# The last layer's weight product joins the order that is planned at build time; the low parts of converted weights move from POOL to DVE

## The chip, the cores and the metric

The kernel runs on one core of a Trainium2 chip. The metric is the device time of one execution in microseconds (us). Three runs of the kernel before took 1078.37, 1080.1 and 1088.2 us, so its median is 1080.1 us. The engines are named as in the profile: PE multiplies matrices (PEld is its weight load), DVE, ACT and POOL do elementwise work, SP issues the DMAs.

## The reference

```
x = attention(q, k, v)            # 4 batches, 8 heads, 576 positions, head size 64, rotary q and k, softmax
x = x / rms(x) * rms_g            # 2304 tokens x 512
x = (silu(x @ w_gate) * (x @ w_val)) @ w_out       # 512 -> 1536 -> 512
x = (((x @ w1) * (x @ w2)) @ w3) @ w_out2          # 512 -> 1024 -> 1024 -> 512
```

The weights arrive as 64-bit floats and are converted on the chip. A product of two float32 matrices is made of three passes (`PASS`): every operand is held as a rounded high part and a low part (the operand less its high part), and the passes are high x high, high x low and low x high.

## The kernel before

**Stages.** The attention (from 0 to about 320 us of the profiled execution) has an order of its own, written out by hand, with the conversion of the first six weight tiles inside it. What follows it is cut here into stages that the text calls B to F.

- B, to 474 us: the gate and value products of the first chunks of tokens (`products_b`, PE line L1059), the gate (`gate_b`), their product with w_out (`second_b`, L1085), and the conversion of 30 more weight tiles (`one_unit`, `convert`, `unit_out`), two per step. A conversion is one ACT operation, two DVE operations (L1117, L1119), one store, and the split into high part (ACT) and low part (`tt` with `pool=True`, on POOL). The rms normalisation of the other tokens (`n_out`) lies in B too.
- C, to 649 us: gate and value products of the other chunks with fewer block products (`block_products`, L1302). Sums and differences of weight blocks are made on POOL (`weights`, `comb`), their splits on ACT and DVE. There are 12 batches of two units.
- D, to 749 us: the product with w_out for those chunks (L1449).
- E, to about 927 us: the products with w1 and w2 (L1302 again), 12 batches of two jobs, 24 jobs. The product of both, u, goes to memory as `uD`.
- F, to the end: first w3 @ w_out2 is made, so that two layers become one. w3 is loaded (`w3_load`), transposed on PE (`w3_trans`, L1552), split, and multiplied with the eight splits `woc` of w_out2 (`w3_prod`, L1563). Then six chunks of u are loaded and split (`load_us`), multiplied with the eight tiles `wp` (L1605, 72 matmuls a chunk), copied out of PSUM and stored.

**The order.** From B to E every operation is handed to `Plan` with its engine, an estimate of its duration and what it reads and writes. At build time `Plan.place` goes through the operations as a list scheduler: PE keeps the order of the program; on ACT, DVE, POOL and SP the operation with the earliest due time goes first among those that are ready. Each engine then has a fixed order. The planner of the kernel before knows nothing that joins DVE and POOL: the two run side by side in its model. Stage F is not in the plan. It is written behind `plan.run()` and `man.close()`, and the framework's own scheduler puts its instructions in order, among the last ones of E as well.

**Buffers.** SBUF is addressed in kilobytes per partition (`mv(address, shape)`), and an address used again waits for the last use of what lay there. PSUM has eight banks that are handed out in turn (`bank`, `pbank`). In E the sums of chunk pairs 0, 1 and 2 lie at `XSA`, `XSB` and `XSC`; the last batch is jobs (3, 1, 1) and (3, 1, 2) and so uses `XSB` and `XSC`, not `XSA`.

**Lines.** L986 and L987 are ACT in `act`, L992 is `tt` (DVE or POOL), L995 is `stt` (DVE), L998 is `dma`, L1117 and L1119 are the two DVE operations of `convert`, L1538 and L1539 are ACT and DVE of stage F's `split`, L885 is a copy in the attention's first steps.

Of the kernel before, what the change touches and what calls it, by code (L numbers as in the profile page):

```python
# [60 lines left out]
SUMS_D, SUMS_E = (72, 78), (194, 200)  # L61
G_AT = (0, 6, 12, 18, 24)
XSC = (84, 90, 96, 182, 188, 72, 78)
ARENAS = ((0, 54), (54, 78), (78, 122), (122, 182), (182, 204))

C_BATCHES = ([[(0, 0), (1, 0)], [(0, 1), (1, 1)]] + [[(f_, 0), (f_, 1)] for f_ in range(2, 10)] + [[(10, 0), (11, 0)], [(10, 1), (11, 1)]])
# [58 lines left out]
class Plan:  # L125
# [4 lines left out]
    def __call__(self, eng, dur, fn, rd=(), wr=(), dep=(), pre=(), due=None, kb=0):  # L130
        o = Op()
        o.eng, o.dur, o.fn, o.kb, o.due, o.pre, o.wr = eng, dur, fn, kb, due, list(pre), wr
        o.i = len(self.ops)
        o.dep = set(dep)
        for acc, w in [(a, 0) for a in rd] + [(a, 1) for a in wr]:
            sp, lo, hi = acc
            if sp not in self.log and isinstance(sp, View):
                for v, log in list(self.log.items()):
                    if isinstance(v, View) and v.lo < sp.hi and sp.lo < v.hi:
                        self.entry.setdefault(sp, set()).update(self.used[v] - {o})  # L140
                        self.over.add(v)
                        del self.log[v]
                        if v.lo < sp.lo or sp.hi < v.hi:
                            self.log[v] = log
            assert sp not in self.over
            if w:
                o.dep |= self.entry.get(sp, set())
            old = self.log.setdefault(sp, [])
            self.used.setdefault(sp, set()).add(o)
            for e in old:  # L150
                if e[0] < hi and lo < e[1] and (w or e[3]) and e[2] is not o:
                    o.dep.add(e[2])
            if w:
                old[:] = [e for e in old if not (lo <= e[0] and e[1] <= hi)]
            old.append((lo, hi, o, w))
        self.ops.append(o)
        return o
# [27 lines left out]
    def place(self, nxt, by, pe):  # L185
        free = dict.fromkeys(("PE", "ACT", "DVE", "POOL", "SP", "X"), 0.0)
        left = {o: len(o.dep) for o in self.ops}
        ready = {e: [] for e in free}
        when = {}
        wire = 0.0  # L190
        self.seq = {e: [] for e in free}
        pe_at = 0

        def release(o):
            when[o] = max([0.0] + [(d.end if o.eng != "X" else d.start) + self.lat(d, o) for d in o.dep])
            ready[o.eng].append(o)

        for o in self.ops:
            if not left[o]:
                release(o)  # L200
        n = 0
        while n < len(self.ops):
            best = None
            for e, r in ready.items():
                if not r:
                    continue
                if e == "PE":
                    o = pe[pe_at]
                    if left[o]:
                        continue  # L210
                    c = (max(free[e], when[o]), o)
                else:
                    t = max(free[e], min(when[o] for o in r))
                    if e == "SP":
                        t = max(t, wire - 3.0)
                    o = min((o for o in r if when[o] <= t), key=lambda o: (by[o], o.i))
                    late = [d for d in r if t < when[d] < t + o.dur and by[d] < by[o] and t + o.dur > max(by[d], when[d] + 0.3)]
                    if late:
                        o = min(late, key=lambda o: when[o])
                        t = when[o]  # L220
                    c = (t, o)
                if best is None or c[0] < best[0]:
                    best = c
            t, o = best
            ready[o.eng].remove(o)
            if o.eng == "PE":
                pe_at += 1
            o.start, o.end = t, t + o.dur
            free[o.eng] = o.end
            if o.kb:  # L230
                wire = max(wire, o.end) + o.kb / 300
                o.end = max(wire, o.end + o.kb / 300) + 1.8
            self.seq[o.eng].append(o)
            n += 1
            for x in nxt[o]:
                left[x] -= 1
                if not left[x]:
                    release(x)
# [28 lines left out]
def kernel(  # L267
# [881 lines left out]
    def unit_out(hi, lo, ph, pl, put, ks, t):  # L1149
        dma(256, put, [ks], lambda: t.ap, [t.part()])  # L1150
        act(hi, [ph], lambda: t.ap, [t.part()], 512)
        tt(lo, [pl], lambda: t.ap, lambda: f(hi()), [t.part(), ph], 512, pool=True)


    NT2 = (NCH - 2) * NR
# [125 lines left out]
    bk = [0]  # L1281
    banks = []

    def bank():
        bk[0] += 1
        i = (bk[0] - 1) % 8
        return (lambda: banks[i][:, 0:CH]), key("bank", i)

    first_c = [None]

# [223 lines left out]
    jobs += [(g, s, P) for g in range(1, NJ // 2) for s in range(2) for P in range(NP2)]  # L1514
    G = {}
    todo = [jobs[k:k + 2] for k in range(0, len(jobs), 2)]
    for batch in todo:
        for g, s, _ in batch:
            if (g, s) not in ws:
                ws[g, s] = wsE(g, s)  # L1520
# [2 lines left out]
            for step in run:  # L1523
                step(i)

    plan.run()
    man.close()


    gtiles, w3s = Ring(G_AT, (DM,)), Ring([a + 2 * i for a in CW for i in range(7)], (512,))  # L1530
    woc, w3T, w3c = {}, {}, {}

    def pbank():
        bk[0] += 1
        return banks[(bk[0] - 1) % 8]

    def split(hi, lo, src, eng=nc.vector):
        nc.scalar.copy(out=hi, in_=src)  # L1538
        eng.tensor_tensor(out=lo, in0=src, in1=f(hi), op=ALU.subtract)  # L1539

    def w3_load(j):
        for h in range(2):
            t = w3c[j, h] = w3s.new().ap
            nc.sync.dma_start(out=t, in_=w3D[:, j, h])

    def w3_trans(j):
        t = w3T[j] = [gtiles.new((NJ, 128), F32R).ap for _ in range(2)]
        for h in range(2):
            src = w3c.pop((j, h))
            p_ = pbank()  # L1550
            for c in range(4):
                nc.tensor.transpose(p_[:, c * 128:(c + 1) * 128], src[:, c * 128:(c + 1) * 128], idn)  # L1552
            split(t[0][:, 4 * h:4 * h + 4], t[1][:, 4 * h:4 * h + 4], p_.rearrange("p (c n) -> p c n", c=4))

    wp = {}

    def w3_prod(j):
        p_ = pbank()
        i = 0
        t = w3T.pop(j)  # L1560
        for c in range(NJ):
            for a, b_ in PASS:
                nc.tensor.matmul(p_, lhsT=t[a][:, c], rhs=woc[c][:, b_], start=(i == 0), stop=(i == 3 * NJ - 1))  # L1563
                i += 1
        o = wp[j] = mv(XSC[j] if j < 7 else XSB[1], (2, 512), F32R).ap
        split_s(o[:, 0], o[:, 1], p_, UP**-2)

    u_ring = Ring(XSB[2:6] + XSA * 4, (2, 2, CH), F32R)

    def load_us(i):  # L1570
        us = []
        for g in range(NJ // 2):
            o = u_ring.new().ap
            nc.sync.dma_start(out=f(o[:, 1]), in_=uD[:, 2 * g:2 * g + 2, i * CH:(i + 1) * CH])
            split(o[:, 0], o[:, 1], f(o[:, 1]))
            us.append(o)
        return us

    for j in range(2):
        w3_load(j)  # L1580
    for j in range(NJ):
        woc[j] = mv(XSA[j] if j < 7 else XSB[0], (3, 512), F32R).ap
        nc.sync.dma_start(out=f(woc[j][:, 2]), in_=woD[:, j])
    for j in range(NJ):
        split(woc[j][:, 0], woc[j][:, 1], f(woc[j][:, 2]))
    w3_trans(0)
    for j in range(NJ):
        if j == NJ - 3:
            nus = load_us(0)
        if j + 2 < NJ:  # L1590
            w3_load(j + 2)
        if j + 1 < NJ:
            w3_trans(j + 1)
        w3_prod(j)


    for i in range(NCH):
        us = nus
        if i + 1 < NCH:
            nus = load_us(i + 1)  # L1600
        ac = [pbank() for _ in range(NR)]
        for j in range(NJ):
            for o in range(NR):
                for s, (a, b_) in enumerate(PASS):
                    nc.tensor.matmul(ac[o], lhsT=us[j // 2][:, a, j % 2, o * 128:(o + 1) * 128], rhs=wp[j][:, b_],  # L1605
                                     start=(j == 0 and s == 0), stop=(j == NJ - 1 and s == 2))
        for o in range(NR):
            t = gtiles.new().ap
            if o == 1:
                nc.vector.tensor_copy(out=t, in_=ac[o])  # L1610
            else:
                nc.scalar.copy(out=t, in_=ac[o])
            g, w = divmod(i * NR + o, 9)
            if w < 8:
                b_, r = 2 * g + w // 4, w % 4
                nc.sync.dma_start(out=out[b_ * S:b_ * S + 512, :].rearrange("(p r) n -> p r n", r=4)[:, r, :], in_=t)
            else:
                for b_ in range(2):
                    e = (2 * g + b_ + 1) * S
                    nc.sync.dma_start(out=out[e - 64:e, :], in_=t[b_ * 64:b_ * 64 + 64, :])  # L1620


# [48 lines left out]
```

## Time and profile before

| | us |
|---|---|
| median of three runs (1078.37 to 1088.2) | 1080.1 |
| profiled execution | 1086.88 |
| its span, first to last instruction | 1085.1 |
| PE busy | 1053.2 (97%) |
| DVE busy | 726.5 (67%) |
| ACT busy | 631.5 (58%) |
| POOL busy | 397.4 (37%) |

The span is what the trace holds; the execution is 1.8 us longer. Busy time is the time in which an engine has an instruction under way, and the rest of the span is idle time. The granted clock is the share of TensorE's full clock (2.4 GHz) that the chip allowed; 0.50 is 1.2 GHz.

### The profile page before, as it was taken

The page shows a single profiled execution, that of the slowest core. Times are in us where ns is not written, and L with a number is a line of the kernel's source. Part 1 is how long each engine was busy: PE and PEld are TensorE (multiplying, and loading weights), DVE is VectorE, ACT ScalarE, POOL GpSimd, SP SyncE. Part 2 cuts the span into 40 slices and gives each one's busy share as a digit, 9 for nine tenths or more (in the row PEclk, how much of TensorE's full clock was granted, in tenths as well). Part 3 has the DMA queues.
Part 4 walks back from the last instruction along what each step waited for, and adds up shares of the span by engine and source line. Part 5 has one row for each costly group of instructions (what it writes and reads, how often), then busy time and mean ns, then how long its engine had stood idle before and what let it go on. Part 6 is the DMA issues. An engine that isn't in the chain of part 4 may idle for free.

```text
span 1085.1 us, 18628 instructions
## 1 busy us (share of the span) xinstructions
PE 1053.2 (97%) x6525; PEld 1017.2 (94%) x6525; DVE 726.5 (67%) x1235; ACT 631.5 (58%) x1414; POOL 397.4 (37%) x509
## 2 busy tenths in 40 slices
PE   7699999999999999999999999999999999899997
PEld 6699999999999899999999999999999999788886
DVE  6999999999987865878787786433745344523220
ACT  4699999898977554557666674323544334322220
POOL 7668897889623444632231230012421110000000
PEclk9899999999999999999999999999999999999999
DMA  6387877777649886369998866653222128304441
GB/s 184 85 214 198 229 186 178 186 193 193 171 158 318 256 283 226 107 200 355 303 303 275 304 211 224 183 162 117 88 69 84 62 88 265 114 1 134 128 146 59
DMA packets 129181, 196.32 MB, mean 181 GB/s; under 512 B 19008, under 2 KB 78016, under 8 KB 129088
## 3 DMA queue, kind: packets, MB, share of 16 engines
q1 hardware_dynamic: 129088, 195.13, 59.5%
q8 instruction: 52, 0.85, 0.3%
q14 instruction: 41, 0.34, 0.1%
HBM read 110.54 MB, written 56.89 MB: 154 GB/s over the span
## 4 chain that ended last, share of the span: by engine, by line
PE 62%; DVE 1%; DMA 1%; issue 1%; ACT 0%; POOL 0%; DVEq 0%; POOLq 0%; ACTq 0%
PE ps L1302 30%; PE ps L1449 9%; PE ps L1605 9%; PE mm L1059 6%; PE ps L1563 4%; PE acc L1085 3%; DVE v L992 1%; DMA v<-x2D 0%; PE ps L1552 0%; DMA v<-uD 0%; DVE v L995 0%; POOL v L992 0%; DMA v<-woD 0%; PE xp L1186 0%; DVE v L1117 0%
## 5 line engine op out<-in xcount | busy, mean ns | idle before, releaser
L1302 PE MATMUL ps<-v 128*128 128x384 f32 x2016 | 350.9, 334 | 0.1
L1302 PEld LDWEIGHTS ps<-v 128*128 128x128 f32 x2016 | 349.3, 188 | 0.8 <-ACT ps L986 0.8
L992 POOL TENSOR_TENSOR v<-v 128x256 f32<-128x256 f32 (+2 forms) x150 | 155.7, 1053 | 400.6 <-DMA v<-x2D 108.5
L986 ACT CAST v<-v 128x256 fp32r<-128x256 f32 (+3 forms) x312 | 151.4, 508 | 149.8 <-DMA v<-uG 37.9
L992 DVE TENSOR_TENSOR v<-v 128x256 fp32r<-128x256 f32 (+3 forms) x282 | 173.6, 641 | 90.2 <-ACT v L986 89.7
L650 PE MATMUL s<-ks,qs 128*128 128x288 f32 x640 | 121.0, 315 | 14.7 <-ACT p L661 13.6
L661 ACT ACTIVATE p<-s,nm 128x576 f32<-128x576 f32 x144 | 107.4, 746 | 19.5 <-DVE nm L655 18.9
L655 DVE TENSOR_REDUCE nm<-s 128x1 f32<-128x576 f32 x144 | 108.0, 751 | 7.4 <-PE s L650 5.5
L1059 PE MATMUL mm<-v 128*128 128x384 f32 x576 | 106.5, 339 | 3.4 <-DVE v L995 2.4
L650 PEld LDWEIGHTS s<-ks,qs 128*128 128x128 f32 x640 | 90.4, 191 | 18.1 <-ACT p L661 16.1
L1059 PEld LDWEIGHTS mm<-v 128*128 128x128 f32 x576 | 101.5, 190 | 4.7 <-DVE v L995 2.6
L1449 PE MATMUL ps<-v 128*128 128x384 f32 x576 | 100.0, 334 | 0.0
L1449 PEld LDWEIGHTS ps<-v 128*128 128x128 f32 x576 | 99.9, 188 | 0.0
L1605 PE MATMUL ps<-v 128*128 128x512 f32 x432 | 98.1, 389 | 0.0
L1605 PEld LDWEIGHTS ps<-v 128*128 128x128 f32 x432 | 81.1, 188 | 16.8
L675 DVE TENSOR_TENSOR pt<-tp,pt 128x512 fp32r<-128x512 f32 x144 | 94.7, 683 | 1.3 <-ACT pt L671 0.6
L992 DVE TENSOR_TENSOR v<-ps,v 128x384 f32<-128x384 f32 x96 | 53.0, 555 | 57.4 <-PE ps L1302 56.1
L986 ACT COPY v<-ps 128x384 f32<-128x384 f32 x120 | 57.2, 479 | 52.3 <-PE ps L1302 50.8
L671 ACT CAST pt<-tp 128x512 fp32r<-128x512 f32 x144 | 82.3, 584 | 1.1 <-PE tp L667 0.2
L667 PE MATMUL tp<-idn,p 128*128 128x128 f32 x576 | 81.9, 274 | 0.9 <-DVE lt L705 0.8
L723 PE MATMUL pv<-pt,vs 128*128 128x288 f32 x512 | 80.9, 300 | 0.1
L723 PEld LDWEIGHTS pv<-pt,vs 128*128 128x128 f32 x512 | 70.9, 188 | 0.3 <-DVE pt L675 0.3
(125 smaller groups left out, 1372.6 us busy)
## 6 DMA issues: line engine op xcount, KB each, us to landing
ks<-xy SPq DMA_DIRECT2D x60, 288.0 KB, 4.9
v<-in_moe_w_dram SPq DMA_DIRECT2D x32, 512.0 KB, 6.2
v<-in_moe_w_out_dram SPq DMA_DIRECT2D x20, 512.0 KB, 6.4
qs<-xy SPq DMA_DIRECT2D x60, 160.0 KB, 2.8
uG<-v SPq DMA_DIRECT2D x24, 384.0 KB, 4.4
v<-uG SPq DMA_DIRECT2D x24, 384.0 KB, 3.8
uD<-v SPq DMA_DIRECT2D x12, 768.0 KB, 3.4
v<-uD SPq DMA_DIRECT2D x24, 384.0 KB, 4.3
```

The costliest lines, as they stand in the source:

```text
L650: nc.tensor.matmul(ps[:, hf, 0:HS], lhsT=l, rhs=r_[:, hf * HS:(hf + 1) * HS], start=(i == 0), stop=(i == n - 1))
L655: nc.vector.tensor_reduce(out=nm, in_=s_ps[p, t][:, :, 0:HS], axis=AX.XY, op=ALU.max, negate=True)
L661: nc.scalar.activation(out=pp.rearrange("p (a b) -> p a b", a=2), in_=s_ps.pop((p, t))[:, :, 0:HS], func=AF.Exp, bias=s_max.pop((p, t)), s ...
L671: lastins["act"] = nc.scalar.copy(out=hi, in_=src)
L675: lastins["dve"] = nc.vector.tensor_tensor(out=lo, in0=src, in1=f(hi), op=ALU.subtract)
L723: nc.tensor.matmul(ps[:, 0:HS], lhsT=l.rearrange("p s d -> p (s d)"), rhs=r, start=(i == 0), stop=(i == 8))
L986: return plan("ACT", act_us(n), lambda: nc.scalar.copy(out=o(), in_=i()), rd, wr)
L992: lambda: eng.tensor_tensor(out=o(), in0=x(), in1=y(), op=op), rd, wr)
L1059: nc.tensor.matmul(p_, lhsT=w.ap[:, a, s, c * 128:(c + 1) * 128], rhs=x.ap[:, b_, c, :], start=(j == 0), stop=(j == 3 * KC - 1))
L1302: nc.tensor.matmul(p_(), lhsT=w[i].ap[:, a, c * 128:(c + 1) * 128], rhs=x[i].ap[:, r, c], start=(first and ch != 1 and n == 0), stop=(n == 5),
L1449: nc.tensor.matmul(ac[o][ch][0](), lhsT=w.ap[:, a, o * 128:(o + 1) * 128], rhs=u.ap[:, b_, ch], start=(j == 0 and s == 0), stop=(j == NF - ...
L1605: nc.tensor.matmul(ac[o], lhsT=us[j // 2][:, a, j % 2, o * 128:(o + 1) * 128], rhs=wp[j][:, b_], start=(j == 0 and s == 0), stop=(j == NJ ...
```

## The change

Three things are changed. The low part of a converted weight tile in stage B (`unit_out`) is made by DVE. The planner has a lock: POOL's operations, and those DVE operations that read SBUF alone, are planned one after the other (`o.lk`, `lock`). Stage F is handed to `Plan` like the other stages, at addresses of its own (`W3R_AT` to `OUT_AT`): the first two loads of w3, its first transposes, and the loads and splits of w_out2 stand ahead of the last batch of E in the program, and the first chunk of u is loaded behind product 5 of 8. The splits of w_out2 are made in place (4 KB in place of 6 KB). The number of matmuls, transposes, splits, loads and stores is the same.

```diff
+W3R_AT, W3T_AT = tuple(194 + 2 * i for i in range(5)), (62, 140, 148)
+WOC_AT, WP_AT = tuple(30 + 4 * i for i in range(8)), (156, 160, 164, 168, 172, 176, 182, 186)
+UF_AT, OUT_AT = (0, 6, 12, 18, 24, 72, 78, 84, 90, 96), (103, 105, 107, 109, 111, 113)
...
+        o.lk = eng == "POOL" or eng == "DVE" and bool(rd) and all(isinstance(a[0], View) for a in rd)
...
-        wire = 0.0
+        wire = lock = 0.0
...
-                    c = (t, o)
+                    c = (max(t, lock) if o.lk else t, o)
...
+            if o.lk:
+                lock = o.end
...
-        tt(lo, [pl], lambda: t.ap, lambda: f(hi()), [t.part(), ph], 512, pool=True)
+        tt(lo, [pl], lambda: t.ap, lambda: f(hi()), [t.part(), ph], 512)
...
+    def split_in(v, n, src, rd, kb):
+        hi, lo = (lambda: v.ap[:, 0]), (lambda: v.ap[:, 1])
+        dma(kb, lambda: f(lo()), [v.part(1, 2)], src, rd)
+        act(hi, [v.part(0, 2)], lambda: f(lo()), [v.part(1, 2)], n)
+        tt(lo, [v.part(1, 2)], lambda: f(lo()), lambda: f(hi()), [v.part()], n)
...
+    for k_, batch in enumerate(todo):
+        if k_ == len(todo) - 1:
+            for j in range(2):
+                w3_load(j)
+            w3_trans(0)
+            for c in range(NJ):
+                split_in(woc[c], 512, lambda c=c: woD[:, c], [key("woD", c)], 256)
...
-    plan.run()
-    man.close()
...
-    for j in range(2):
-        w3_load(j)
...
+    nus = None
     for j in range(NJ):
-        if j == NJ - 3:
-            nus = load_us(0)
         if j + 2 < NJ:
             w3_load(j + 2)
         if j + 1 < NJ:
             w3_trans(j + 1)
         w3_prod(j)
+        if j == NJ - 3:
+            nus = load_us(0)
...
+    plan.run()
+    man.close()
```

What is left out here rewrites `w3_load`, `w3_trans`, `w3_prod`, `load_us` and the loop over the six chunks from direct calls into calls of `plan`, `act`, `tt`, `stt` and `dma`, with the same operations on the same engines.

## Rows read from the trace of the kernel before

**Rows 1.** The page: busy time of each engine, share of the span, instructions

```profile
PE 1053.2 (97%) x6525; PEld 1017.2 (94%) x6525; DVE 726.5 (67%) x1235; ACT 631.5 (58%) x1414; POOL 397.4 (37%) x509
```

**Rows 2.** Stretches: start:end, length, busy PE, PEld, DVE, ACT, POOL, clock, DMA

```profile
320.00:360.00 40.00, 39.17 (x231) 38.20 (x230) 32.45 (x62) 26.31 (x61) 12.38 (x9) 1.00 0.81 263
360.00:372.00 12.00, 9.62 (x52) 9.35 (x51) 10.99 (x16) 6.22 (x14) 7.50 (x4) 0.86 0.87 276
372.00:430.00 58.00, 58.00 (x345) 57.93 (x344) 33.10 (x48) 29.64 (x55) 25.38 (x22) 1.00 0.85 271
...
474.00:649.00 175.00, 175.00 (x1011) 175.00 (x1010) 139.75 (x273) 116.55 (x262) 48.33 (x52) 1.00 0.87 292
...
1079.40:1085.10 5.70, 0.00 (x0) 0.00 (x0) 0.00 (x0) 0.59 (x1) 0.00 (x0) 0.74 0.46 139
```

**Rows 3.** What PE waited for: total us, times, longest

```profile
PE s L650 <- ACT p L661: 13.6, 7, 10.6
PE ps L1563 <- ACT v L1538: 4.0, 1, 4.0
PE mm L1059 <- DVE v L995: 2.4, 1, 2.4
```

**Rows 4.** Instructions in time, DVE and POOL, 13 to 32 us

```profile
13.47 0.81 DVE L885 CAST qs<-xy 64x512 fp32r<-64x512 f32 x1
...
21.59 10.50 DVE L885 CAST qs<-xy 64x512 fp32r<-64x512 f32 x1
...
28.92 2.88 POOL L551 TENSOR_TENSOR rot<-rot,rtmp 128x384 f32<-128x384 f32 x3
```

**Rows 5.** The chain that ended last, E into F: start, us, what

```profile
920.01 4.18 DMA v<-uD
...
929.14 1.36 DVE v L995
...
930.53 0.59 ACT v L1538
...
931.17 5.33 PE ps L1563 x14
...
951.48 5.46 PE ps L1563 x24
```

**Rows 6.** A stretch behind the gap of E into F, columns as before

```profile
933.00:934.00 1.00, 1.00 (x4) 0.81 (x3) 0.00 (x0) 0.00 (x0) 0.00 (x0) 0.50 0.44 166
```

**Rows 7.** Instructions by line, DVE, 895 to 916 us: busy, mean ns, idle before

```profile
L1539 DVE TENSOR_TENSOR v<-v 128x512 fp32r<-128x512 f32 x8 | 5.5, 692 | 10.3 <-ACT v L1538 10.3
```

**Rows 8.** Instructions in time, the last split of w_out2 in E

```profile
914.13 0.69 DVE L1539 TENSOR_TENSOR v<-v 128x512 fp32r<-128x512 f32 x1 [0.38 <-ACT v L1538]
```

**Rows 9.** Instructions in time, DVE, POOL and PE, 360 to 377 us

```profile
360.13 2.91 POOL L992 TENSOR_TENSOR v<-v 128x512 fp32r<-128x512 f32 x2 [11.00 <-ACT v L986]
...
362.00 1.60 DVE L1119 SCALAR_TENSOR_TENSOR v<-v 128x512 uint32<-128x512 uint32 x1
...
364.85 1.49 DVE L1117 TENSOR_SCALAR v<-v 128x512 uint32<-128x512 uint32 x1
...
367.38 0.41 DVE L1117 TENSOR_SCALAR v<-v 128x512 uint32<-128x512 uint32 x1
...
367.51 6.01 PE L1059 MATMUL mm<-v 128*128 128x384 f32 x24 [2.38 <-DVE v L995]
367.72 0.68 DVE L1119 SCALAR_TENSOR_TENSOR v<-v 128x512 uint32<-128x512 uint32 x1
```

**Rows 10.** The chain again, products of B at the full clock

```profile
384.50 4.17 PE mm L1059 x24
```

**Rows 11.** Instructions by line, 320 to 430 us on POOL, 372 to 430 us on DVE

```profile
L992 POOL TENSOR_TENSOR v<-v 128x512 fp32r<-128x512 f32 x28 | 40.3, 1451 | 59.4 <-ACT v L986 58.1 <-DMA v<-partD 1.3
...
L1119 DVE SCALAR_TENSOR_TENSOR v<-v 128x512 uint32<-128x512 uint32 x15 | 13.3, 901 | 2.5 <-ACT v L411 2.3
L1117 DVE TENSOR_SCALAR v<-v 128x512 uint32<-128x512 uint32 x13 | 9.6, 753 | 5.4 <-DMA v<-in_moe_w_out_dram 4.4 <-DMA v<-in_moe_w_val_dram 1.0
```

More of the change, by code (lines that the diff above doesn't have):

```diff
@@ L1282, with bank @@
     banks = []
-    def bank():
+    def bank(n=CH):
         bk[0] += 1
         i = (bk[0] - 1) % 8
-        return (lambda: banks[i][:, 0:CH]), key("bank", i)
+        return (lambda: banks[i][:, 0:n]), key("bank", i)
     first_c = [None]
@@ L1516 @@
     todo = [jobs[k:k + 2] for k in range(0, len(jobs), 2)]
-    for batch in todo:
+    w3r, w3t, ur, outr = Ring(W3R_AT, (512,)), Ring(W3T_AT, (2, NJ, 128), F32R), Ring(UF_AT, (2, 2, CH), F32R), Ring(OUT_AT, (DM,))
+    woc, wp = [mv(a, (2, 512), F32R) for a in WOC_AT], [mv(a, (2, 512), F32R) for a in WP_AT]
+    w3c, w3T = {}, {}
+    def split_in(v, n, src, rd, kb):
[3 more added lines that the diff above has]
+        tt(lo, [v.part(1, 2)], lambda: f(lo()), lambda: f(hi()), [v.part()], n)
@@ new lines, in w3_load, with w3_trans, go @@
+    def w3_load(j):
+        for h in range(2):
+            t = w3c[j, h] = w3r.new()
+            dma(256, lambda t=t: t.ap, [t.part()], lambda h=h: w3D[:, j, h], [key("w3D", 2 * j + h)])
+    def w3_trans(j):
+        t = w3T[j] = w3t.new()
+        for h in range(2):
+            src, (p_, sl) = w3c.pop((j, h)), bank(512)
+            def go(src=src, p_=p_):
+                for c in range(4):
+                    nc.tensor.transpose(p_()[:, c * 128:(c + 1) * 128], src.ap[:, c * 128:(c + 1) * 128], idn)
+            plan("PE", 0.44, go, [src.part()], [sl])
+            split_v(lambda h=h: t.ap[:, 0, 4 * h:4 * h + 4], t.part(h, 4), lambda h=h: t.ap[:, 1, 4 * h:4 * h + 4], t.part(2 + h, 4),
+                    lambda p_=p_: p_().rearrange("p (c n) -> p c n", c=4), sl, 512)
@@ new lines, in w3_prod, with go @@
+    def w3_prod(j):
+        (p_, sl), t, o = bank(512), w3T.pop(j), wp[j]
+        def go():
+            i = 0
+            for c in range(NJ):
+                for a, b_ in PASS:
+                    nc.tensor.matmul(p_(), lhsT=t.ap[:, a, c], rhs=woc[c].ap[:, b_], start=(i == 0), stop=(i == 3 * NJ - 1))
+                    i += 1
+        plan("PE", 24 * 0.2267, go, [t.part()] + [v.part() for v in woc], [sl])
+        act(lambda: o.ap[:, 0], [o.part(0, 2)], p_, [sl], 512, scale=UP**-2)
+        stt(lambda: o.ap[:, 1], [o.part(1, 2)], p_, UP**-2, lambda: f(o.ap[:, 0]), [sl, o.part(0, 2)], 512, op1=ALU.subtract)
@@ new lines, in load_us @@
+    def load_us(i):
+        us = [ur.new() for _ in range(NJ // 2)]
+        for g, v in enumerate(us):
+            split_in(v, 2 * CH, lambda g=g: uD[:, 2 * g:2 * g + 2, i * CH:(i + 1) * CH], [key("uD", 3 * g + i // 2)], 384)
+        return us
+    for k_, batch in enumerate(todo):
[3 more added lines that the diff above has]
+            w3_trans(0)
+            for c in range(NJ):
+                split_in(woc[c], 512, lambda c=c: woD[:, c], [key("woD", c)], 256)
@@ L1524 @@
                 step(i)
-    plan.run()
-    man.close()
[L1530 to L1577, printed above, removed]
-    for j in range(2):
-        w3_load(j)
-    for j in range(NJ):
[L1582 to L1587, printed above, removed]
-        if j == NJ - 3:
-            nus = load_us(0)
+    nus = None
+    for j in range(NJ):
         if j + 2 < NJ:
@@ L1600, with go @@
             nus = load_us(i + 1)
-        ac = [pbank() for _ in range(NR)]
+        ac = [bank(512) for _ in range(NR)]
         for j in range(NJ):
             for o in range(NR):
-                for s, (a, b_) in enumerate(PASS):
-                    nc.tensor.matmul(ac[o], lhsT=us[j // 2][:, a, j % 2, o * 128:(o + 1) * 128], rhs=wp[j][:, b_],
-                                     start=(j == 0 and s == 0), stop=(j == NJ - 1 and s == 2))
+                def go(j=j, o=o, u=us[j // 2], p_=ac[o][0]):
+                    for s, (a, b_) in enumerate(PASS):
+                        nc.tensor.matmul(p_(), lhsT=u.ap[:, a, j % 2, o * 128:(o + 1) * 128], rhs=wp[j].ap[:, b_],
+                                         start=(j == 0 and s == 0), stop=(j == NJ - 1 and s == 2))
+                plan("PE", 3 * 0.2267, go, [us[j // 2].part(), wp[j].part()], [ac[o][1]])
         for o in range(NR):
-            t = gtiles.new().ap
+            t, (p_, sl) = outr.new(), ac[o]
             if o == 1:
-                nc.vector.tensor_copy(out=t, in_=ac[o])
+                plan("DVE", dve_us(512), lambda t=t, p_=p_: nc.vector.tensor_copy(out=t.ap, in_=p_()), [sl], [t.part()])
             else:
-                nc.scalar.copy(out=t, in_=ac[o])
+                act(lambda t=t: t.ap, [t.part()], p_, [sl], 512)
             g, w = divmod(i * NR + o, 9)
@@ L1615 @@
                 b_, r = 2 * g + w // 4, w % 4
-                nc.sync.dma_start(out=out[b_ * S:b_ * S + 512, :].rearrange("(p r) n -> p r n", r=4)[:, r, :], in_=t)
+                dma(256, lambda b_=b_, r=r: out[b_ * S:b_ * S + 512, :].rearrange("(p r) n -> p r n", r=4)[:, r, :], [], lambda t=t: t.ap, [t.part()])
             else:
@@ L1619 @@
                     e = (2 * g + b_ + 1) * S
-                    nc.sync.dma_start(out=out[e - 64:e, :], in_=t[b_ * 64:b_ * 64 + 64, :])
+                    dma(128, lambda e=e: out[e - 64:e, :], [], lambda t=t, b_=b_: t.ap[b_ * 64:b_ * 64 + 64, :], [t.part()])
+    plan.run()
+    man.close()
 _INS = ['q', 'k', 'v', 'moe_w_gate', 'moe_w_val', 'moe_w_out', 'moe_rms_g',
```

## The prediction

> **What bounds the kernel now.** I read the busy times first. PE works 1053.2 of 1085.1 us [rows 1], so 31.9 us are all that can be gained without fewer or faster matmuls, and the change has the same matmuls. The second view is what PE waited for [rows 3]: a long wait of 10.6 us in the attention, 4.0 us once at L1563 and 2.4 us once at L1059; every other wait is under 1.5 us. Third, the busy time by stretches [rows 2] shows where an edit can pay: from 372 to 430 us, and through all of stage C, PE is busy in every microsecond. A better order cannot help there, it can only hurt. What the change touches and what is idle is the gap from E into F, the gap in B near 365 us, and the 5.7 us behind the last matmul.
>
> The profiled execution took 1086.88 us, 6.8 more than the median. The trace has a reason that lies outside the change: a DVE copy that takes 0.81 us at 13.47 takes 10.50 us at 21.59, and ends when POOL's run of rotary products ends, at 31.80 [rows 4]; PE's wait of 10.6 us is its price [rows 3]. Without these 9.7 us the execution would be 1077.2 us, close to the two lower runs (1078.4 and 1080.1), and the third run, 1088.2, looks like the profiled one. That is in the attention, whose order stays. I make the sum on 1086.88 and carry the difference over to the median.
>
> **Edit 1: stage F joins the plan.** The gap: the framework put the load and the four splits of the first u chunk among the last instructions of E. The chain goes from a load of `uD` that lands at 924.19 through DVE's last operation of E (1.36 us, at 929.14) to the ACT split of transposed w3 at 930.53, and only then PE starts at 931.17 [rows 5]; that is the 4.0 us of [rows 3]. Behind the gap the granted clock is 0.50, the lower of the two levels, in the stretch shown [rows 6], and 14 matmuls take 5.33 us where 24 at the full clock take 5.46 [rows 5]: 14 x 5.46 / 24 = 3.19, so 2.1 us more are lost. Price of the gap: 4.0 + 2.1 = 6.1 us.
>
> In the changed program the first transposes, and the loads and splits of w_out2, stand ahead of the last batch, and the planner sees their due times, while the u chunk is due some 50 us later (eight products of 5.46 us stand before its use). Does the last batch hide them? The eight low parts are 8 x 0.69 = 5.5 us of DVE [rows 7], and in the kernel before they already lie under E: the last one ended at 914.82 [rows 8], 11 us before E's matmuls did. The same loads need the same buffers free (those of job (3, 1, 0), done one batch before the end), so I see no reason for them to be later. If that cover is gone, PE waits at L1563 again. I take the whole 6.1 us as gained; bounds: nothing gained, and 6.1.
>
> The moved steps issue 16 + 8 + 24 loads and 20 stores on SP, as before. SP waits in order: a load that is planned behind a store of `uD` waits for the DVE operation of 1.36 us that writes it. The loads for F's start stand in front of E's last two stores by due time, so I cost this at 0 and cover one such operation, 1.4 us, by the range. The tail behind the last matmul (one ACT copy of 0.59 us, then stores, to 5.7 us [rows 2]) has the same operations: 0.
>
> **Edit 2: the low parts of converted weights on DVE.** In the trace POOL makes 28 of these in stage B at 1.45 us each [rows 11]. DVE did the same shape, two SBUF inputs, in 0.69 [rows 7]; 28 x 0.69 = 19.4 us go to an engine that is busy 32.45 of 40 us, then 10.99 of 12, then 33.10 of 58 [rows 2]. Against that stands what POOL's operations cost DVE: L1117 takes 0.41 when POOL is quiet and 1.49 at 364.85, L1119 0.68 and 1.60 [rows 9]. Near the gap three DVE operations are held so (the third like the first): 1.08 + 0.92 + 1.08 = 3.1 us. The three POOL operations of the two rows' stretch become 3 x 0.69 = 2.1 us on DVE. Net: DVE reaches the gate operation, on which PE waits [rows 9], 1.0 us earlier. Over 372 to 430 us the relief on L1119 and L1117 alone is 15 x (0.90 - 0.68) + 13 x (0.75 - 0.41) = 7.7 us [rows 11], against 18 more operations of 0.69, 12.4: DVE rises from 33.1 to about 38 of 58 us, and does not become the bound.
>
> The Trainium skill, Perfetto Trace Analysis, section Optimizing Scalar/DVE Operations, says that with a saturated DVE it may make sense to hand work to GpSimd, though the two share an SBUF port and it might not help. The first half speaks against this edit: by it alone the gap would grow by 2.1 us. The rows hold with its second half: what POOL did cost DVE more there (3.1) than doing it would (2.1).
>
> The gap itself cost 2.38 us of waiting, and then 24 matmuls took 6.01 us [rows 9] where others take 4.17 [rows 10]: 1.8 us of clock, 4.2 in all. The gain of 1.0 us is the floor that I count on; the order of DVE is planned anew and the gate may stand further ahead, and then all 4.2 are gained. I take 2.0, near the floor since both the wait and the clock have to go for more. Bounds: 4.2 gained, or 2.1 lost (no relief).
>
> **Edit 3: the lock in the planner.** It issues nothing. It changes the order on DVE, ACT, POOL and SP from B to E. PE has no idle time to give back in C [rows 2], so below it is bounded by about zero; above, by a new gap at the price of the present one, 6.1 us. I take 0: PE's own order is fixed by the program, and real waits of DVE for POOL are in the trace already, unplanned for, without harm to PE in C.
>
> **Sum.** 6.1 + 2.0 + 0 = 8.1 us. The profiled execution would go from 1086.88 to 1078.8 with the long attention wait, 1069.1 without; the median from 1080.1 to **1072 us**, 0.75% less.
>
> **Rivals.**
> 1. *Only one of the two gaps closes.* If B stays as it is: 1080.1 - 6.1 = 1074.0. If F's start is late again, say because a u split is still planned ahead of the w3 split (the change would not do what it says): 1080.1 - 2.0 = 1078. For it: one DVE operation of 1.36 us in front suffices [rows 5]. Against: the due times.
> 2. *Both gaps close wholly.* 6.1 + 4.2 = 10.3: 1069.8. With a run or two near the lower end of the present spread (1.7 below the median) the measured time would be 1068, over 1% faster. For it: the planner now foresees the contention that made DVE late. Against: DVE is full from 360 to 372.
> 3. *Slower: the lock bends the order in C and E.* DVE and POOL together are busy 139.75 + 48.33 = 188 us of 175 in C [rows 2]. If most of DVE's part read SBUF alone, the planner would see a queue that does not fit, plan ever later, and put operations that feed PE behind others. The price: one operation per batch that is about 1.0 us late (a DVE operation behind POOL's [rows 9]), 24 batches in C and E, 24 us, less the 8.1: 1096. It decides from the point where DVE's planned part and POOL's fill a batch of C; 35 us of 175 are free on DVE now. Against: the PSUM readers are not locked, and due times, not start times, rank the queue.
> 4. *The attention's long wait decides.* If more than half of the new runs hold that wait, the median is 1088.2 - 8.1 = 1080, no change. The trace and the runs show it in about two of four executions.
>
> **How the numbers follow.** My forecast (1071 to 1076, the gap of F and a part of B's) has a chance of 0.46; rival 1 at its worse half (F not gained) 0.10; rival 2 0.19; rival 3, and smaller mishaps of its kind, 0.12; rival 4 0.13. The range: down to 1065, which is rival 2 (1069.8) with the spread of runs and the bounds' uncertainty; up to 1083, which holds rivals 1 and 4 and one lost operation more. Left out are rival 3 and a little of 2. One per cent, about what a measurement of this kernel can tell from no change, is 10.8 us, or 1069.3 and 1090.9. Faster by more needs both gaps wholly and a good median: 0.2. Slower by more needs rival 3: 0.1. The rest, 0.7, is within.
>
> **What would show it.** Step by step in the profile after: the wait of L1563's PE for ACT is gone, and the first 24 matmuls of F take about 5.46 us; no granted clock under 1.00 between 920 and 940. In B, L1117 near 0.42 and L1119 near 0.69 us, 30 operations of 128x512 on DVE at 0.69, and POOL empty until the weight differences. PE's wait for the gate of B shorter than 2.4 us. C still without idle time on PE. I am wrong if PE shows new waits in C to E for DVE or ACT (the lock), or if DVE's first gate operations of B come later than now (the moved low parts), or if F's first product waits for a split of w_out2.

## The result, and the profile after

The changed kernel takes 1065.35 us (median of six runs, 1063.88 to 1073.41) against 1078.44 for the kernel before in the same comparison: 13.1 us less, a ratio of 0.9881 with a 95% interval of 0.9832 to 0.9930. The time lies at the low edge of the range (1065 to 1083); the forecast of 8.1 us less was too small.

The profiled execution took 1073.41 us, 13.5 less than the profiled one of before (1086.88). Both hold the long DVE copy in the attention, so the two traces can be set side by side. First the busy times on the page of the kernel after, which answer to [rows 1].

```profile
span 1071.6 us, 18577 instructions
PE 1047.7 (98%) x6525; PEld 1014.0 (95%) x6525; DVE 724.7 (68%) x1265; ACT 632.0 (59%) x1414; POOL 351.3 (33%) x479
```

PE's idle time fell from 31.9 to 23.9 us, and its busy time by 5.5 though it has the same 6525 matmuls. By the prediction's own two prices, 1.8 and 2.1 us, 3.9 of these 5.5 are time at the lower clock behind the two gaps; the rest was not separated. POOL lost 30 instructions, DVE gained 30 and is busy no longer than before. The stretches of the kernel after, columns as in [rows 2]:

```profile
320.00:360.00 40.00, 40.00 (x242) 39.91 (x241) 33.68 (x74) 27.79 (x64) 2.11 (x2) 1.00 0.83 277
360.00:372.00 12.00, 12.00 (x80) 11.93 (x79) 11.96 (x23) 7.88 (x16) 0.00 (x0) 1.00 0.98 311
372.00:430.00 58.00, 58.00 (x341) 57.96 (x340) 37.22 (x68) 31.19 (x61) 6.36 (x8) 1.00 0.77 252
...
474.00:649.00 175.00, 175.00 (x1011) 175.00 (x1011) 141.19 (x274) 118.73 (x267) 45.08 (x51) 1.00 0.86 290
...
926.00:981.00 55.00, 55.00 (x265) 45.90 (x264) 17.12 (x25) 14.60 (x25) 0.00 (x0) 1.00 0.27 87
```

PE is busy through all of them at the full clock. From 360 to 372 us DVE has no pause (11.96 of 12), and still PE does not wait for it. What PE waited for, against [rows 3], is now in the attention alone (total us, times, longest):

```profile
PE s L656 <- ACT p L667: 12.6, 4, 10.6
PE warm L873 <- POOL idn masks.py:199: 1.4, 1, 1.4
```

The chain of the kernel after from E into F, against [rows 5] (start, us, what):

```profile
904.22 14.59 PE ps L1308 x84
918.80 0.87 PE ps L1545 x8
919.68 5.47 PE ps L1557 x24
```

E's last batch, eight transposes and the first product of w3 follow each other without a break, and the 24 matmuls of that product take the 5.47 us of the full clock.

For a balance I read four lengths from each trace: B from its first gate product to the first matmul of C, C, E with the start of F (from E's first matmul to the first matmul of the six chunks), and the tail.

| us | before | after | less |
|---|---|---|---|
| B | 166.4 | 160.4 | 5.9 |
| C | 174.7 | 174.7 | 0.0 |
| E with F's start | 232.6 | 225.5 | 7.1 |
| tail behind the last matmul's start | 6.1 | 5.4 | 0.8 |

(The last column is taken before rounding.) With 0.3 lost ahead of B, that is the 13.5. The tail lies between 5.1 and 6.1 in all kernels below, whatever their edits, so the 0.8 is not the change's.

### The profile page after: what moved, and what is told of

The parts are those of the page before. It is cut to its first block, busy times and chain, and to the rows that moved or that the text cites. A ratio compares the mean times of both kernels' runs of the same rounds, so it can differ in the third digit from the quotient of the medians.

```text
span 1071.6 us, 18577 instructions
## 1 busy us (share of the span) xinstructions
PE 1047.7 (98%) x6525; PEld 1014.0 (95%) x6525; DVE 724.7 (68%) x1265; ACT 632.0 (59%) x1414; POOL 351.3 (33%) x479
## 4 chain that ended last, share of the span: by engine, by line
PE 91%; DVE 4%; POOL 2%; DMA 1%; SPq 1%; issue 1%; ACT 0%; DVEq 0%; POOLq 0%; ACTq 0%
PE ps L1308 33%; PE mm L1065 9%; PE ps L1455 9%; PE ps L1602 9%; PE s L656 6%; PE pv L729 6%; PE tp L673 5%; PE acc L1091 4%; PE ps L1557 4%; PE lp L703 1%; PE qtp L590 1%; PE op L743 1%; DVE qs L891 1%; DVE nm L661 1%; PE ps L1545 1%; POOL rtmp L543 1%
## 5 line engine op out<-in xcount | busy, mean ns | idle before, releaser
L998 DVE TENSOR_TENSOR v<-v 128x256 fp32r<-128x256 f32 (+3 forms) x344 | 218.0, 657 | 144.7 <-ACT v L992 143.5
L992 ACT CAST v<-v 128x256 fp32r<-128x256 f32 (+3 forms) x344 | 175.8, 534 | 182.7 <-DMA v<-uD 41.7
L998 POOL TENSOR_TENSOR v<-v 128x256 f32<-128x256 f32 (+1 forms) x120 | 109.3, 926 | 431.5 <-DVE v L998 204.3
L992 ACT COPY v<-ps 128x384 f32<-128x384 f32 (+1 forms) x132 | 64.6, 490 | 94.2 <-PE ps L1308 51.0
L1065 PE MATMUL mm<-v 128*128 128x384 f32 x576 | 104.2, 335 | 0.1
L998 DVE TENSOR_TENSOR v<-ps,v 128x384 f32<-128x384 f32 (+1 forms) x112 | 63.4, 573 | 56.3 <-PE ps L1308 53.7
```

Source lines behind the costliest of these rows:

```text
L992: return plan("ACT", act_us(n), lambda: nc.scalar.copy(out=o(), in_=i()), rd, wr)
L998: lambda: eng.tensor_tensor(out=o(), in0=x(), in1=y(), op=op), rd, wr)
L1065: nc.tensor.matmul(p_, lhsT=w.ap[:, a, s, c * 128:(c + 1) * 128], rhs=x.ap[:, b_, c, :], start=(j == 0), stop=(j == 3 * KC - 1))
```

## The experiments

The edits, by the names used below. **DVE**: `pool=True` removed in `unit_out`. **Lock**: `o.lk`, `lock` in the planner. **F**: stage F in the plan. All numbers of one line come from the kernel's own trace and comparison.

| kernel | edits | median us | ratio to before, 95% | B | E with F's start |
|---|---|---|---|---|---|
| before | none | 1078.4 | | 166.4 | 232.6 |
| f_only | F | 1070.75 | 0.9929 (0.9909 to 0.9948) | 166.3 | 225.8 |
| dve_only | DVE | 1073.5 | 0.9941 (0.9913 to 0.9970) | 160.4 | 232.8 |
| lock_only | lock | 1076.04 | 0.9983 (0.9957 to 1.0008) | 163.8 | 232.5 |
| f_dve | F, DVE | 1068.32 | 0.9907 (0.9872 to 0.9942) | 160.4 | 225.7 |
| f_lock | F, lock | 1067.78 | 0.9921 (0.9894 to 0.9947) | 163.8 | 225.5 |
| dve_lock | DVE, lock | 1072.13 | 0.9954 (0.9921 to 0.9988) | 160.4 | 232.9 |
| after | all | 1065.35 | 0.9881 (0.9832 to 0.9930) | 160.4 | 225.5 |

**One edit at a time, and two.** The diffs against the kernel after are these lines, one or both; against the kernel before, the same the other way round.

```diff
-        o.lk = eng == "POOL" or eng == "DVE" and bool(rd) and all(isinstance(a[0], View) for a in rd)
+        o.lk = False
...
-        tt(lo, [pl], lambda: t.ap, lambda: f(hi()), [t.part(), ph], 512)
+        tt(lo, [pl], lambda: t.ap, lambda: f(hi()), [t.part(), ph], 512, pool=True)
```

f_only: 

> Stage F in the plan, but no lock, and the low parts still on POOL. Two lengths are read from the trace: B from its first gate product to the first matmul of C (166.5 us before, 160.6 after), and E with the start of F, from E's first matmul to the first matmul of the six chunks (232.5 before, 225.5 after). Theory: F in the plan alone closes its gap, E with F's start 225.5 us, B unchanged at 166.5, time about 7 us below the kernel before (1071.5). Rival: the lock sets the order at E's end too, then E with F's start stays above 228 us.

f_dve: 

> Stage F in the plan and the low parts on DVE, no lock. Theory (POOL's operations hold DVE in B, and moving them ends that): B 160.6 to 162 us, E with F's start 225.5, time as after the whole change (1065.4). Rival (the lock's order closes the gap in B): B stays at 165 or more, time 1070 to 1072.

f_lock: 

> Stage F in the plan and the lock, the low parts still on POOL. Theory (moving them closes B's gap): B 165 to 167 us, time 1070 to 1072. Rival (the planned order closes it, since the planner now foresees the waits): B 161 to 162, time 1065 to 1067.

dve_lock: 

> The low parts on DVE and the lock, stage F outside the plan as before. Theory: B 160.6 us, E with F's start 232.5, the gap of about 4 us in front of F's first product still there, time about 6 us below the kernel before (1072.5). Rival (the two parts meet, and the shorter B shifts what F finds): E with F's start differs from 232.5 by more than 1.5 us.

dve_only: 

> The kernel before with one edit: the low parts of the converted weights on DVE. Theory (POOL held DVE): B 160.6 to 162 us where it was 166.5, no operation L1117 or L1119 of DVE above 1 us in it, time about 5 to 6 us below the kernel before. Rival (the order decides): B 165 or more.

lock_only: 

> The kernel before with one edit: the lock in the planner. Theory: nothing to gain, B 165 to 167 us, C, D and E as before, time within 2 us. Rival 1 (order closes B's gap): B 161 to 162. Rival 2 of the prediction (the lock bends the order): new waits of PE in C or E, one us per batch, 12 us or more longer.

 (The second rival named there is the third of the prediction.)

The table answers them. E with F's start is 225.5 to 225.8 with F in the plan and 232.5 to 232.9 without, whatever the other two edits are. B is 160.4 with the low parts on DVE, lock or not; with the lock alone it is 163.8. So the lock closes 2.5 of B's 5.9 us while POOL still makes the low parts, and nothing once DVE does. That middle value is neither the theory's (165 to 167) nor the rival's (161 to 162). (In dve_only the longest L1119 of B takes 1.21 us, so not every operation stayed under the 1 us that was expected.) The waits of PE from B on in f_lock show what is left:

```profile
PE mm L1065 <- DVE v L1001: 1.7, 1, 1.7
PE mm L1065 <- ACT v L992: 0.5, 1, 0.5
PE mm L1065 <- DVE v L998: 0.3, 1, 0.3
```

The wait for the gate shrank from 2.4 to 1.7 us and did not go. Most of the 2.5 us is clock. The 24 matmuls behind that wait, first in f_only and then in f_lock:

```profile
358.55 6.01 PE L1065 MATMUL mm<-v 128*128 128x384 f32 x24 [2.40 <-DVE v L1001]
```

```profile
357.12 4.45 PE L1065 MATMUL mm<-v 128*128 128x384 f32 x24 [1.73 <-DVE v L1001]
```

In f_only the granted clock behind the wait is 0.50 (360 to 361 us); in f_lock it is 1.00 there, and 1.000 on average over the whole execution. C is 174.7 to 174.9 in all of these but dve_only (175.3): the lock bends nothing there. Its own worth in the whole change is not resolved: f_dve has the B of after and an E with F's start that is 0.3 us longer, and their intervals overlap.

**Is it the holding of DVE by POOL?** dve_pool keeps everything of the kernel after and gives POOL its work back as well.

```diff
         tt(lo, [pl], lambda: t.ap, lambda: f(hi()), [t.part(), ph], 512)
+        tt(lo, [pl], lambda: t.ap, lambda: f(hi()), [t.part(), ph], 512, pool=True)
```

> The changed kernel, in which POOL writes the low part of each converted weight tile of B once more behind DVE, the same values to the same place. Theory (POOL's operations hold DVE, and that made B long): B is 164 us or more where it is 160.5, L1123 and L1125 of DVE have operations above 1 us again. Rival (the new order of DVE made B short, the holding did not matter): B stays within 161.5 us. POOL writes the same later, so products that need a low part wait for it too; such waits of PE are counted apart.

B became 171.9 us where it was 160.4, the median 1076.64 (0.9974, 0.9959 to 0.9989). DVE's two operations of a conversion, 320 to 440 us, in dve_pool (busy, mean ns, idle before):

```profile
L1125 DVE SCALAR_TENSOR_TENSOR v<-v 128x512 uint32<-128x512 uint32 x28 | 26.3, 949 | 1.3 <-ACT v L417 0.4 <-DMA wsG<-v 0.3 <-DVE v L1123 0.2
...
L1123 DVE TENSOR_SCALAR v<-v 128x512 uint32<-128x512 uint32 x25 | 18.7, 754 | 4.2 <-DMA v<-in_moe_w_out_dram 3.0 <-DMA v<-in_moe_w_gate_dram 1.2
```

and in the kernel after, 320 to 430 us:

```profile
L1125 DVE SCALAR_TENSOR_TENSOR v<-v 128x512 uint32<-128x512 uint32 x28 | 19.1, 706 | 2.2 <-ACT v L417 2.1
L998 DVE TENSOR_TENSOR v<-v 128x512 fp32r<-128x512 f32 x28 | 19.0, 688 | 7.5 <-ACT v L992 7.5
...
L1123 DVE TENSOR_SCALAR v<-v 128x512 uint32<-128x512 uint32 x25 | 10.3, 424 | 0.0
```

With POOL's operations the same DVE instructions take 949 and 754 ns, without them 706 and 424. What PE waited for in dve_pool, 300 to 500 us:

```profile
PE mm L1065 <- POOL v L998: 6.1, 3, 2.9
PE mm L1065 <- DVE v L1001: 1.3, 2, 1.0
PE mm L1065 <- DVE v L998: 0.4, 1, 0.4
PE acc L1091 <- DVE v L998: 0.4, 1, 0.4
```

6.1 of the 11.5 us that B grew are waits for POOL's late second writing, which the experiment adds by itself. The clock falls once in B, behind the longest of these waits (columns as in [rows 2]):

```profile
419.00:422.00 3.00, 3.00 (x11) 3.00 (x11) 0.62 (x2) 0.00 (x0) 1.52 (x1) 0.50 0.62 236
```

These 3 us at half the clock cost 1.5, which is the experiment's own as well. The other 3.9 hold 2.1 us of waits for DVE; 1.8 are not placed. The holding is shown, and that DVE's waits come back with it; that the full 5.9 us are its price is not. Moving the work also changes DVE's order, and how much of the gain is order was not separated.

**What made the gap of E into F?** The prediction laid it to the load and splits of the first u chunk, which the framework put among E's last instructions. u_late moves them in the program of the kernel before.

```diff
     for j in range(NJ):
-        if j == NJ - 3:
-            nus = load_us(0)
...
         w3_prod(j)
+    nus = load_us(0)
```

> The kernel before with one edit: the first u chunk is loaded and split behind the last w3 product, not among the first of F. Theory (the load and splits of u, standing among E's last instructions, make PE wait): the 4.0 us wait in front of F's first product falls under 1 us, E with F's start 226 to 228 us instead of 232.5. Rival (the first transposes of w3 come too late whatever stands beside them): a wait of 2 us or more remains, 229 to 232. A new wait may come ahead of the first chunk, if its splits are then late; it is counted apart.

Nothing changed: the wait is 4.0 us, E with F's start 232.6, the ratio 0.9982 (0.9955 to 1.0008). ACT's rows of u_late show why the edit tells little, and something else:

```profile
912.58 0.83 ACT L1538 CAST v<-v 128x768 fp32r<-128x768 f32 x1 [1.59 <-DMA v<-uD]
...
918.25 0.84 ACT L1538 CAST v<-v 128x768 fp32r<-128x768 f32 x1 [1.11 <-DMA v<-uD]
919.70 1.07 ACT L1538 CAST v<-ps 128x512 fp32r<-128x512 f32 x2 [0.62 <-DVE v L995]
922.24 2.05 ACT L1538 CAST v<-ps 128x512 fp32r<-128x512 f32 x4 [1.47 <-DVE v L995]
```

The framework put u's splits (128x768) where they had been, so the theory went untested here. But ACT stood idle for 1.47 us ahead of the last row, and DVE's L995, the last operation of E, ended that wait, though a split of transposed w3 reads nothing of it. What joins them is an address. In the kernel before, the transposed w3 lies in the ring `G_AT`, and its first tile takes addresses 0 and 6. At 0 lie the sums of job (3, 0, 2), which E's last DVE operation reads.

t_late takes the kernel after and puts the transposes behind the last batch again, at their free address.

```diff
-            w3_trans(0)
             for c in range(NJ):
                 split_in(woc[c], 512, lambda c=c: woD[:, c], [key("woD", c)], 256)
...
     nus = None
+    w3_trans(0)
```

> The changed kernel, but the first transposes of w3 stand behind the last batch of E, not ahead of it. Theory (what counts is that the plan keeps u's splits away): F's first product waits about 2 us for the split of its transposes and no more, E with F's start 227 to 228 us. Rival (what counts is that the transposes stand one batch, 14.6 us, earlier): the wait is 3 us or more and the clock falls behind it, 229 to 232 us.

Neither: no wait from B to the end, E with F's start 225.7, median 1063.92 (0.9873, 0.9813 to 0.9933), which can't be told from the changed kernel. No worth of the earlier place of the transposes shows. Then the address alone, both ways. t_free is the kernel before with the first tile of transposed w3 elsewhere; the later tiles move up the ring by two places:

```diff
-        t = w3T[j] = [gtiles.new((NJ, 128), F32R).ap for _ in range(2)]
+        t = w3T[j] = [(gtiles.new((NJ, 128), F32R) if j else mv(a, (NJ, 128), F32R)).ap for a in (194, 198)]
```

> The kernel before with one edit: the first transposed tile of w3 lies at 194 and 198, where nothing of E is left, and not at 0 and 6, where the last batch of E still reads the sums of job (3, 0, 2). New theory (the split waits for that buffer until E's last DVE operation): the 4.0 us wait in front of F's first product falls under 0.5 us, E with F's start 225 to 226.5 us instead of 232, B unchanged at 166.3, time 6 to 7 us below the kernel before. Rival (the framework's order alone makes the gap, as the prediction had it): still 3 us or more of waiting.

The wait is gone and E with F's start is 226.5 us: 6 of the 7.1 us by one address. The order did not stay as it was, though. With the address free, the framework put the first matmuls of w3's product among E's last ones, as two rows of PE show:

```profile
912.69 0.48 PE L1563 MATMUL ps<-v 128*128 128x512 f32 x1
913.01 3.31 PE L1302 MATMUL ps<-v 128*128 128x384 f32 x18
```

So the address is what was edited, and part of the way in which it helps is the order that it allows. The median is 1071.61, the ratio 0.9932 (0.9907 to 0.9958); B is 166.3. The waits of PE from B on in t_free, the gap of B among them:

```profile
PE mm L1059 <- DVE v L995: 2.4, 1, 2.4
PE mm L1059 <- ACT v L986: 0.5, 1, 0.5
PE mm L1059 <- DVE v L992: 0.3, 1, 0.3
PE ps L1302 <- ACT ps L986: 0.2, 1, 0.2
```

t_on_e is t_late with that tile at 0.

```diff
-W3R_AT, W3T_AT = tuple(194 + 2 * i for i in range(5)), (62, 140, 148)
+W3R_AT, W3T_AT = tuple(194 + 2 * i for i in range(5)), (0, 140, 148)
...
-UF_AT, OUT_AT = (0, 6, 12, 18, 24, 72, 78, 84, 90, 96), (103, 105, 107, 109, 111, 113)
+UF_AT, OUT_AT = (12, 18, 24, 72, 78, 84, 90, 96, 0, 6), (103, 105, 107, 109, 111, 113)
```

> The changed kernel with the first transposes behind the last batch, as in t_late, and with the first transposed tile of w3 at address 0, where E's last operations still read. The u chunks take the same addresses in another turn. New theory (the buffer makes the gap): PE waits 3 to 5 us again for ACT in front of F's first product, E with F's start 229 to 233 us, though the whole of F is planned; time 5 to 7 us above t_late. Rival (the plan's order hides it): as t_late, 225.2 us.

The wait came back smaller than expected: 1.9 us, E with F's start 228.3, 2.6 above t_late; the median is 1067.56 (0.9896, 0.9870 to 0.9921). Its instructions in time:

```profile
909.99 1.07 ACT L992 CAST v<-ps 128x512 fp32r<-128x512 f32 x2 [2.84 <-PE ps L1545]
910.19 1.36 DVE L1001 SCALAR_TENSOR_TENSOR v<-v 128x1152 f32<-128x1152 f32 x1
...
911.68 1.09 ACT L992 CAST v<-ps 128x512 fp32r<-128x512 f32 x2
...
912.33 0.73 PE L1557 MATMUL ps<-v 128*128 128x512 f32 x2 [1.94 <-ACT v L992]
```

ACT's second pair starts once DVE's last operation of E has ended at 911.55. So the address makes the wait. Its size goes with how late E's last DVE operation is: here it ends 3.1 us behind E's last matmul (908.48, where the transposes start), in the kernel before 5.0 us behind it (930.50 and 925.49), and 16 transposes fill a part.

**Can the long copy in the attention be avoided?** q_act takes the kernel after and gives ACT the copy of pair 1.

```diff
-        nc.vector.tensor_copy(out=qst[p][64:128, 0, 0:512], in_=ys[0:64, 0:512])
+        (nc.scalar.copy if p else nc.vector.tensor_copy)(out=qst[p][64:128, 0, 0:512], in_=ys[0:64, 0:512])
```

> The changed kernel with the attention's one copy of 64 x 512 that at times takes 10.5 us on DVE (at 21 us of the profile, while POOL runs its rotary products) made by ACT. Theory (that copy, held until POOL's queue is empty, makes the longer of the two groups of runs, some 8 us apart): no run above 1067 us, median 1063 to 1065.5, against 1065.35 for the changed kernel. Rival (another DVE operation is then held in its place): runs at 1071 to 1073 are still there.

The rival held: median 1072.65 (1065.59 to 1076.5), ratio 0.9922 (0.9890 to 0.9954), and so no better than the changed kernel. In q_act's trace the first of the next two copies of that kind is held instead, for 8.41 of these 9.30 us:

```profile
23.18 9.30 DVE L887 CAST ks<-xy 64x576 fp32r<-64x576 f32 x2
```

In f_only, whose profiled execution has no long hold, the copy of pair 1 reads:

```profile
21.38 0.72 DVE L891 CAST qs<-xy 64x512 fp32r<-64x512 f32 x1
```

No version tried here is shown to be faster than the changed kernel.

## Why the prediction came out as it did

**What bounds the kernel**: right. C did not gain (174.7 in both), and most of what was gained lay in the two gaps and the clock behind them; 1.7 us lay in smaller waits of B, which I had left out.

**Edit 1, 6.1 us**: the size was nearly right (7.1 measured, 6.8 for F alone), the reason half wrong. I laid the gap to the order of the framework's scheduler and counted on the planner's due times. The runs show an address: t_free closes the gap without the planner, and t_on_e brings a part of it back in the plan. That the plan puts F's tiles at addresses of their own was part of the change, but no term of my sum. The planner does not even keep u's splits away from E's end; in t_late they stand there too, and no one waits. The price of the clock was seen rightly in the chain [rows 5]; what I missed is that the ACT split there waited for an operation that it does not read. Its cover, the eight splits under E's last batch, held.

**Edit 2, 2.0 us**: this is the term that was mis-sized; it measured 5.9, above my bound of 4.2. The direction was right. So was the kind of cause (POOL holds DVE), as far as dve_pool shows it. That POOL costs DVE more than the work itself is not borne out over the whole stretch (below). I weighed three held operations next to the gap, but holding had gathered since 320 us. DVE of the kernel before, 320 to 430 us (busy, mean ns, idle before), and one place early in it:

```profile
L1119 DVE SCALAR_TENSOR_TENSOR v<-v 128x512 uint32<-128x512 uint32 x28 | 25.8, 933 | 4.0 <-ACT v L411 3.6
L1117 DVE TENSOR_SCALAR v<-v 128x512 uint32<-128x512 uint32 x25 | 17.8, 724 | 5.4 <-DMA v<-in_moe_w_out_dram 4.4 <-DMA v<-in_moe_w_val_dram 1.0
```

```profile
323.56 2.91 DVE L1119 SCALAR_TENSOR_TENSOR v<-v 128x512 uint32<-128x512 uint32 x2
```

Two of L1119 took 2.91 us where two without POOL take 1.4. Over the stretch the mean of L1119 fell from 933 to 706 ns, that of L1117 from 724 to 424: 28 x 0.227 + 25 x 0.300 = 13.9 us of relief against 19.0 of new work. So DVE has about 5 us more to do there, and the gate still comes in time; whether by the holds that are gone ahead of it or by the new order is not separated. What I left out are the small waits of PE near 330 to 338 us, 0.4 and 0.3 the longest. PE's order up to the gap is the same in both kernels, so one place of it can be compared, 12 matmuls of `second_b` behind these waits, before and after:

```profile
341.54 2.24 PE L1085 MATMUL acc<-v 128*128 128x384 f32 x12
```

```profile
340.08 2.24 PE L1091 MATMUL acc<-v 128*128 128x384 f32 x12
```

From B's first gate product to here it is 33.8 and 32.0 us: 1.7 less. From here to C it is 132.6 and 128.4: 4.2 less, just the price that I had put on the gap and its clock. The whole gap closed where I counted on half of it, and the stretch ahead of it, which I had put at nothing, gave 1.7 more.

The rule of the Trainium skill that spoke against this edit (Perfetto Trace Analysis, Optimizing Scalar/DVE Operations, its first half) is not borne out here: DVE was busy 10.99 of 12 us from 360 to 372, and taking work back from POOL made B 5.9 us shorter.

**Edit 3, 0**: right with the other two to within 0.3 us, the difference of f_dve's lengths from those of after. Alone it is worth 2.5 us in B, which I had not seen: I looked for idle time in C, and the gap of B was there to be shortened.

**Rivals.** The second (both gaps close wholly) is what happened, with 0.19; its 1069.8 was too high for the reason above, and by 1.7 us because the median of the kernel before was 1078.44 in this comparison and not 1080.1. The third (the lock bends C and E) is refuted by lock_only and by C's length in f_lock. The fourth did not decide the medians: two of the six runs of the kernel after are the long ones (1071.9 and 1073.41; the profiled one, 1073.41, shows the wait). My chance of 0.2 for more than 1% faster followed from the cap of 10.3 us that I had set on the gain, and that cap rested on edit 2's bound; 13.1 were gained. That the time still lies in the range, by 0.35 us, is luck: the room that I had left for the spread of runs took up what the terms missed (1.0 in edit 1, 3.9 in edit 2) and those 1.7.

## What to carry to other kernels

When an operation waits for one that it does not read, look at the address of what it writes: one tile laid over a late reader cost 6 us here, partly through the order that it forced. Look for holding by the mean duration of the same DVE operation with and without POOL at work, over the whole stretch in which both run and not only where the wait shows. But do not decide between POOL and DVE by the sum of DVE's work alone: it grew by about 5 us over the stretch here, and B became 5.9 us shorter. What counts is when DVE reaches the operations that PE waits for. And take a cap on a gain from all the waits of a stage, the small ones and their clock too.

## What the runs showed of the hardware

The long copy in the attention was not expected to be that stubborn. In the kernel after it is held for 10.52 us while POOL starts and ends twelve rotary instructions; the chain of waits and POOL's rows:

```profile
21.16 10.52 DVE qs L891
```

```profile
22.39 2.90 POOL L537 TENSOR_TENSOR rot<-raw,cos 128x384 f32<-128x384 f32 x3
25.24 3.31 POOL L543 TENSOR_TENSOR rtmp<-raw,sin 128x192 f32<-128x192 f32 x6
28.50 2.90 POOL L557 TENSOR_TENSOR rot<-rot,rtmp 128x384 f32<-128x384 f32 x3
```

DVE does not get through between one POOL instruction and the next. In B the two engines take turns: in the kernel before, POOL makes three low parts without a pause, and DVE's operations end one by one among them.

```profile
324.19 5.14 POOL L992 TENSOR_TENSOR v<-v 128x512 fp32r<-128x512 f32 x3
```

```profile
326.39 1.78 DVE L995 SCALAR_TENSOR_TENSOR v<-v,st,g 128x512 f32<-128x512 f32 x1
```

A held L1119 or L1117 in B is late by no more than about one POOL operation [rows 9]. It can go the other way too: at 369.13 one POOL operation takes 3.09 us (its mean is 1.45) while DVE runs L1117 and L1119 without a pause. Nor is the stage what decides. In f_only, where the copy that starts at 21.38 gets through in 0.72 us, DVE takes turns with the same twelve POOL instructions; in f_dve, whose copy was not held either, DVE's L442 was held for 4.48 us at 169.69, over several POOL instructions:

```profile
29.75 1.39 DVE L437 SCALAR_TENSOR_TENSOR v<-v 128x512 uint32<-128x512 uint32 x1
```

```profile
169.69 4.48 DVE L442 SCALAR_TENSOR_TENSOR v<-v 128x512 uint32<-128x512 uint32 x1
```

What decides between the two is open. It also means that the copy of pair 1 is not the only thing that makes a run of these kernels long: f_dve's profiled execution (1070.33) is one of its two longer runs.

The Trainium skill, SBUF — State Buffer, section "SBUF: two separate sides", says that the engine that starts first holds the port pair that DVE and GpSimd share for one whole instruction. B's rows agree. That section does not say which engine comes next, and in the attention DVE's copy stood back for twelve POOL instructions.
